# Scores of a batch cut into 14 pieces that fill their PSUM banks, in five bursts for six, and attention pairs released at four per MLP chunk

## The chip, the cores and the metric

The kernel runs on one core of one Trainium2 chip. The metric is the device time of one execution, in microseconds. Durations and waits come from one profiled execution of each kernel, taken by the hardware profiler.

## The reference

Attention with 16 extra "beacon" keys ahead of each head's own keys (8 batches, 8 heads, 576 queries, head size 64), and behind it an MLP with a squared relu over the 4608 tokens that come out of it:

```python
k_all = np.concatenate([beacon_k, k], axis=2)          # 592 keys
v_all = np.concatenate([beacon_v, v], axis=2)
scores = scale * np.matmul(q, k_all.transpose(0, 1, 3, 2))
causal[:, Nb:] = np.triu(np.ones((S, S), dtype=bool), k=1)
scores = np.where(causal, -1000000000.0, scores)
a = np.exp(scores - scores.max(-1, keepdims=True))
a /= a.sum(-1, keepdims=True) + 1e-09
x = np.matmul(a, v_all)          # then tokens x 512
h = x @ w_in                     # 512 -> 2048
r = np.maximum(h, 0.0)
out = (r * r) @ w_out            # 2048 -> 512
```

## The kernel before

The work of a batch is four head pairs; pair p = 4b + pr. The 592 keys make five key blocks c of 128 (the last has 80), and the queries five tiles t, of 112, 128, 128, 128 and 80 rows, so that block c meets the tiles from c on. Scores are made transposed, keys on the partitions: one matmul of TensorE per key block and head, with 64 rows of weights, and the two heads of a pair side by side in the upper and the lower half of the array. One such couple is called a step below. A tuple `(c, t0, t1, col)` in `WHOLE` is a step: key block c, queries t0 to t1, at column `col` of the PSUM bank (one bank for each head). The steps of one bank pair are a piece; ScalarE takes its exponential into the pair's tile `pt` in one instruction (L768). VectorE then masks the diagonal blocks with triangles from `tri` by a minimum (L783, and L787 for the block of 80), TensorE multiplies the probabilities by v (30 matmuls of 65 columns, L803; the 65th column gives the sum), and VectorE divides into `xn` (L818, L819).

Scores come in bursts: `SIZES` says how many pieces one scheduled operation takes, each with a bank pair of its own. In batch 0, split in two phases (`SPLIT`), it is one piece, in batch 1 two pieces, and from batch 2 on the 16 pieces of a batch make six bursts (3, 3, 3, 3, 2, 2).

When all four pairs of a batch are done, `xn` is turned into `xT` by five DMA transposes that SyncE issues (L850; batch 0 uses TensorE). The MLP takes tokens in nine chunks of 512: chunk j needs xT of the batches up to j, chunk 8 of batch 7. A chunk is 64 matmuls of 512 columns by w_in (L931), relu on ScalarE or VectorE (L948, L950), a square on VectorE (L957) and 64 matmuls by w_out (L968), which ScalarE copies out (L437) and SyncE stores (L991).

From batch 3 on, q and k are loaded by SyncE (L484, L483 for the beacons), cast by GpSimd, and turned into `qT` and `kT` by DMA transposes of SyncE (L516). The transposes, the loads and the stores stand in one queue. `qT`, `kT`, `xn` and the cast v have two buffers each, `pt` four.

The order of instructions on every engine is fixed when the kernel is built: the class `Order` plays the program through with assumed costs and always takes the operation with the lowest `prio` that may go. Attention comes ahead of the MLP, except that a pair is held back by its `gate` until the MLP has come far enough:

```python
mlp_chunk_us = 27.7
LEAD, PACE = -0.4, 0.225
return o.progress >= mlp_chunk_us * (LEAD + PACE * (p - HP))
```

Here `progress` is the MLP's TensorE time already given out, and HP is 4.

Of the kernel before, what the change touches and what calls it, by code (L numbers as in the profile page):

```python
# [10 lines left out]
BF16 = mybir.dt.bfloat16  # L11
AF = mybir.ActivationFunctionType
# [117 lines left out]
class Order:  # L130
# [180 lines left out]
def kernel(  # L311
# [29 lines left out]
    def sb(name, shape, dt):  # L341
        return pool.tile(shape, dt, name=name)

    NSTG, NPT, RB = 8, 4, 4
# [22 lines left out]
    pt = [sb(f"pt{i}", [128, 2, 2048], BF16) for i in range(NPT)]  # L367
# [7 lines left out]
    tri = sb("tri", [128, 4, 128], BF16)  # L375
# [8 lines left out]
    def act(n):  # L384
        return 0.066 + n / 1200.0
# [17 lines left out]
    add = order.add  # L403
# [8 lines left out]

    def add_pad(i):
        def emit(e):
            for lo, hi in ((928, 1024), (1440, 1536), (1824, 2048)):
                nc.vector.memset(pt[i][:, :, lo:hi], 0.0)

        return add(f"pad{i}", "DVE", 0.5, emit, prio=100.0 * i)
# [1 line left out]
    pads = [add_pad(i) for i in range(NPT)]  # L420

    def emit_tri(e):
        for i in range(4):
            nc.gpsimd.affine_select(out=tri[:, i, :], in_=tri[:, i, :], compare_op=ALU.is_ge, fill=0.0,
                                    base=Nb if i == 0 else 0, pattern=[[1, 128]], channel_multiplier=-1)
# [26 lines left out]
    def t_start(t):  # L452
        return max(0, 128 * t - Nb)
# [219 lines left out]
            self.lo = t_start(tiles[0])  # L673
            self.hi = t_start(tiles[-1]) + t_rows(tiles[-1])

    whole_off = {}
    for t in range(NT):
        for c in range(t + 1):
            whole_off[c, t] = ((t_start(t) if t < 4 else 1360) if c == 0 else
                               1744 if c == 4 else 512 * c + 128 * (t - c))  # L680
# [8 lines left out]
    SPLIT = [  # L689
        Phase(  # L690
            pieces=[([(0, 0, 240, 0), (1, 112, 240, 240)], 0, 368)],
            diag=(0, 240, 0, 2), last=None, tiles=range(0, 2), off={(0, 0): 0, (0, 1): 112, (1, 1): 240}),
        Phase(
            pieces=[
# [3 lines left out]
            ],  # L698
            diag=(512, 512, 2, 2), last=848, tiles=range(2, NT),
            off={(2, 2): 512, (2, 3): 640, (2, 4): 768, (4, 4): 848, (3, 3): 1024, (3, 4): 1152,  # L700
                 (0, 2): 1232, (0, 3): 1360, (1, 2): 1536, (1, 3): 1664, (1, 4): 1792, (0, 4): 1872}),
    ]
# [31 lines left out]
    def add_scores(pairs, n, sizes):  # L734

        work = [(x, i, piece) for x in pairs for i, piece in enumerate(phases(x.b)[n].pieces)]
        exps = {x.p: [] for x in pairs}
        at = 0
        for size in sizes:
            group = work[at:at + size]  # L740
            at += size
            prio = 100.0 * group[0][0].p + 1000.0 * n + group[0][1]
            cols = sum(t1 - t0 for _, _, (mms, _, _) in group for _, t0, t1, _ in mms)
            owners = list({x.p: x for x, _, _ in group}.values())
            box = {}

            def emit_qk(e, group=group, box=box):
                for k, (x, _, (mms, _, _)) in enumerate(group):
                    st = pair(box["qk"], k)
                    for c, t0, t1, col in mms:  # L750
                        for hj in range(2):
                            hp = slice(64 * hj, 64 * hj + 64)
                            nc.tensor.matmul(  # L753
                                st[:, hj, col:col + t1 - t0],
                                kT[x.b % 2][hp, x.pr, 128 * c:128 * c + 128],
                                qT[x.b % 2][hp, x.pr, t0:t1],
                                start=True, stop=True,
                            )

            qk = add(f"qk{group[0][0].p}.{n}.{group[0][1]}", "PE", cols / 2400.0, emit_qk, prio=prio,  # L760
                     deps=[d for x in owners for d in x.qk_deps + [x.take_pt]],
                     take=("ps", "late" if b < NSPLIT and n else "strip", [2] * size), gate=owners[0].gate, mode="rows")
            box["qk"] = qk
            for x in owners:
                qk_ops[x.p].append(qk)
            for k, (x, i, (_, off, width)) in enumerate(group):
                def emit_exp(e, off=off, width=width, k=k, x=x, box=box):
                    nc.scalar.activation(pt[x.take_pt.held[0]][:, :, off:off + width],  # L768
                                         pair(box["qk"], k)[:, :, 0:width], AF.Exp, bias=0.0, scale=scale)

                exps[x.p].append(add(f"exp{x.p}.{n}.{i}", "ACT", act(2 * width), emit_exp, prio=prio + 0.1 * k,
                                     deps=[qk], give=(qk, k)))
# [234 lines left out]
    late = []  # L1007
    for b in range(B):
        lp = 10.0 * b
        if b < NPE:  # L1010
            add_strided(b, lp - 200.0 if b == 0 else lp)
        if NPE <= b < NPE + 2:
            add_zero(b)
        v_loads[b] = []
        for n, (x, c) in enumerate(([] if b < NPE else nat) + [("v", c) for c in range(NT)]):
            behind, sync = [], []
            if x == "v" and b == 0:
                if c == 0:
                    sync = [strided[0][HP - 3, "q"]]
            elif x == "v" and b == 1 and c == 0:  # L1020
                behind = [strided[1][HP - 1, "q"]]
            elif b == 2 and n == 0:
                sync = [w_ops["out", 3]]
            add_load(b, x, c, lp + 0.1 * n, behind, sync)
            if x == "v":
                v_loads[b].append(load_chain[-1])
        if b >= NPE:
            add_trans(b, "k", lp - 5.0)
            add_trans(b, "q", lp - 5.1)
        if b == 0:  # L1030
            add_weights()
        if b == 1:
            add_weights_out()
        pairs = [add_pair(b, pr) for pr in range(HP)]
        if b < NSPLIT:
            for x in pairs:
                for n, ph in enumerate(phases(b)):
                    add_scores([x], n, [1] * len(ph.pieces))
        else:
            add_scores(pairs, 0, SIZES[b])  # L1040
# [48 lines left out]
```

## Time and profile before

| | |
|---|---|
| median of 3 runs | 343.65 us (343.54 to 343.87) |
| the profiled execution | 344.22 us |
| its span, first to last instruction | 342.4 us |
| TensorE matmuls busy | 325.1 us, 95% |
| ScalarE busy | 195.0 us, 57% |
| VectorE busy | 160.3 us, 47% |
| GpSimd busy | 81.1 us, 24% |
| matmuls of scores (L753) | 400 |
| granted TensorE clock | 1.0 |

Engines are PE (matmuls), PEld (weight loads, which overlap PE), DVE (VectorE), ACT (ScalarE), POOL (GpSimd) and SP (SyncE; with a q, its queue of DMA issues). A row of the timeline gives a start and a length in microseconds, the engine, the line, what is written and read, and how many instructions were merged; in brackets the idle time before it and what ended it. A matmul's length contains the time that its result takes to leave the array, so matmuls behind one another overlap in their rows, and the starts tell the pace. A row of the groups gives busy time and the mean length of one in ns, then the idle time before. In the waits it is who waited for whom: sum in us, times, the longest. A row of the stretches has the stretch and its length, the busy time and count of PE, PEld, DVE, ACT and POOL, the granted clock, the DMA engines' share and GB/s. A few records of matmuls are missing.

### The profile page before, as it was taken

Reading aid. Unit: us, or ns where it says so; the run is one execution under the profiler, and the core shown is the slowest. Engines: PE = TensorE matmul, PEld = TensorE weight load, DVE = VectorE, ACT = ScalarE, POOL = GpSimd, SP = SyncE. Lnnn points to the kernel's source line nnn. Section 1 sums busy time; section 2 is a strip of 40 time slices with the busy share of each in tenths; the row PEclk is TensorE's granted clock in tenths of the full one; section 3 lists DMA queues with packets and bytes.
Section 4 is the critical chain, followed back from the end, with each engine's and each line's share of the span. In section 5 each row is a group of like instructions: output and inputs, shape, how many; then the busy total and the mean of one; then the engine's idle time right before and its main releaser. Section 6 shows DMA issues by size and latency. Waiting matters only on the chain.

```text
span 342.4 us, 7074 instructions
## 1 busy us (share of the span) xinstructions
PE 325.1 (95%) x2838; PEld 175.7 (51%) x2876; DVE 160.3 (47%) x323; ACT 195.0 (57%) x301; POOL 81.1 (24%) x129
## 2 busy tenths in 40 slices
PE   2999999999999999999999799999999999999995
PEld 2677665454544544453557574444544444444442
DVE  6788978177425842385524483287403202301400
ACT  3987873588358564577554754597326326515611
POOL 6545802516124222423241126020000000000000
PEclk9999999999999999999999999999999999999999
DMA  9999999699979996999999889980041011011002
GB/s 166 197 205 221 206 204 208 134 252 204 188 164 215 197 199 145 255 188 224 133 209 220 184 177 207 219 170 24 15 117 63 0 61 63 0 61 63 0 29 93
DMA packets 139472, 50.33 MB, mean 147 GB/s; under 512 B 125808, under 2 KB 134512, under 8 KB 139440
## 3 DMA queue, kind: packets, MB, share of 16 engines
q1 hardware_dynamic: 129856, 40.91, 58.1%
q0 software_dynamic: 9376, 8.69, 15.5%
q8 instruction: 22, 0.36, 0.5%
q10 hardware_dynamic: 208, 0.29, 0.3%
q14 instruction: 10, 0.08, 0.1%
HBM read 37.22 MB, written 9.44 MB: 136 GB/s over the span
## 4 chain that ended last, share of the span: by engine, by line
PE 66%; DMA 19%; SPq 7%; DVE 4%; issue 2%; POOL 2%; ACT 1%; POOLq 0%; DVEq 0%; ACTq 0%
PE ps L931 28%; PE ps L968 26%; PE ps L803 5%; SPq L850 5%; PE ps L753 5%; DMA kT<-qk_area 5%; DMA stg<-in_k_dram 4%; DMA bks<-in_beacon_k_dram 3%; DMA stg<-in_v_dram 3%; DVE g L957 2%; DMA stg<-in_q_dram 1%; DMA qk_area<-in_q_dram 1%; SPq L484 1%; POOL w_in L892 1%; PE ps L635 1%
## 5 line engine op out<-in xcount | busy, mean ns | idle before, releaser
L931 PE MATMUL ps<-xT,w_in 128*128 128x512 bf16 (+3 forms) x688 | 134.3, 340 | 1.1 <-DMA xT<-xn 0.2
L968 PE MATMUL ps<-w_out,g 128*128 128x512 bf16 x554 | 127.9, 379 | 1.1 <-issue 0.2
L768 ACT ACTIVATE pt<-ps 128x832 bf16<-128x832 f32 (+4 forms) x128 | 102.9, 872 | 28.6 <-PE ps L753 28.5
L931 PEld LDWEIGHTS <-w_in 128*128 128x128 bf16 x704 | 64.9, 98 | 57.8 <-issue 7.7
L957 DVE TENSOR_TENSOR g<-g 128x1024 bf16<-128x1024 bf16 (+2 forms) x80 | 53.6, 673 | 76.9 <-ACT g L948 75.6
L948 ACT ACTIVATE g<-ps 128x512 bf16<-128x512 f32 (+2 forms) x117 | 66.3, 567 | 39.9 <-PE ps L931 39.2
L968 PEld LDWEIGHTS <-g 128*128 128x128 bf16 x576 | 54.1, 98 | 64.1 <-issue 2.9
L437 ACT COPY osb<-ps 128x512 f32<-128x512 f32 x36 | 21.3, 591 | 65.0 <-PE ps L968 60.4
L439 POOL CAST vb<-stg 128x512 bf16<-128x512 f32 (+1 forms) x36 | 24.3, 684 | 84.3 <-DMA stg<-in_v_dram 39.9
L439 POOL CAST qk_area<-stg 128x512 bf16<-128x512 f32 (+2 forms) x50 | 32.1, 645 | 50.6 <-DMA stg<-in_q_dram 33.8
L783 DVE TENSOR_TENSOR pt<-pt,tri 128x1024 bf16<-128x1024 bf16 (+1 forms) x36 | 23.9, 667 | 31.3 <-ACT pt L768 31.3
L803 PEld LDWEIGHTS <-pt 128*128 128x128 bf16 (+1 forms) x960 | 33.6, 98 | 7.6 <-issue 1.2
L950 DVE TENSOR_SCALAR g<-ps 128x512 bf16<-128x512 f32 (+2 forms) x43 | 25.7, 600 | 24.9 <-PE ps L931 24.5
L803 PE MATMUL ps<-vb,pt 128*128 128x65 bf16 (+1 forms) x960 | 34.9, 194 | 1.3 <-DVE pt L783 0.5
L753 PE MATMUL ps<-qT,kT 64*128 64x80 bf16 (+7 forms) x400 | 33.5, 282 | 2.6 <-DMA kT<-qk_area 2.1
L819 DVE TENSOR_TENSOR xn<-ps,rcp 128x640 bf16<-128x640 f32 (+2 forms) x36 | 27.0, 750 | 1.5 <-DVE rcp L818 0.2
L753 PEld LDWEIGHTS <-kT 64*128 64x128 bf16 x400 | 13.5, 96 | 23.2 <-issue 15.4
L818 DVE RECIPROCAL rcp<-ps 128x10 f32<-128x10 f32 (+2 forms) x36 | 7.5, 208 | 23.1 <-PE ps L803 23.0
L437 ACT COPY qT<-ps 128x576 bf16<-128x576 bf16 x12 | 7.5, 640 | 6.4 <-PE ps L635 5.0
L439 DVE COPY kT<-ps 128x576 bf16<-128x576 bf16 x12 | 8.9, 751 | 2.8 <-PE ps L638 1.9
L787 DVE TENSOR_TENSOR pt<-pt,tri 80x160 bf16<-80x160 bf16 x32 | 10.0, 312 | 0.0
L635 PE MATMUL ps<-ident,sparek 96*128 96x96 bf16 x18 | 1.5, 229 | 6.0 <-DVE sparek L439 6.0
(49 smaller groups left out, 71.7 us busy)
## 6 DMA issues: line engine op xcount, KB each, us to landing
out_dram<-osb SPq DMA_DIRECT2D x17, 512.0 KB, 3.3
stg<-in_v_dram SPq DMA_DIRECT2D x21, 256.0 KB, 5.0
stg<-in_q_dram SPq DMA_DIRECT2D x20, 256.0 KB, 4.7
stg<-in_k_dram SPq DMA_DIRECT2D x15, 256.0 KB, 5.1
w_in<-in_moe_w_in_dram POOLq DMA_DIRECT2D x4, 512.0 KB, 8.2
w_out<-in_moe_w_out_dram POOLq DMA_DIRECT2D x4, 512.0 KB, 10.9
stg<-in_v_dram SPq DMA_DIRECT2D x7, 224.0 KB, 4.2
qk_area<-in_k_dram POOLq DMA_DIRECT2D x4, 288.0 KB, 12.7
```

Of the source, the lines that this page charges most:

```text
L437: nc.scalar.copy(dst, src)
L439: eng[e].tensor_copy(dst, src)
L753: nc.tensor.matmul(st[:, hj, col:col + t1 - t0], kT[x.b % 2][hp, x.pr, 128 * c:128 * c + 128], qT[x.b % 2][hp, x.pr, t0:t1], start=True, s ...
L768: nc.scalar.activation(pt[x.take_pt.held[0]][:, :, off:off + width], pair(box["qk"], k)[:, :, 0:width], AF.Exp, bias=0.0, scale=scale)
L783: nc.vector.tensor_tensor(out=d, in0=d, in1=tri[:, m0:m0 + m, :][:, None].to_broadcast([128, 2, m, 128]), op=ALU.min)
L803: nc.tensor.matmul(a[:, hj, (t - tl[0]) * (D + 1):(t - tl[0] + 1) * (D + 1)], P[0:rr, hj, o:o + 128], vb[b % 2][0:rr, c, h, :], start=(c = ...
L819: nc.vector.tensor_tensor(out=xn[b % 2].rearrange("p t (h d) -> p h t d", d=D)[:, 2 * pr:2 * pr + 2, tl[0]:tl[0] + nt], in0=a[:, :, :, 0:D ...
L931: nc.tensor.matmul(h[:, lo - spans[0][0]:hi - spans[0][0]], w_in_sb[:, mc, ft * 128:(ft + 1) * 128], xT[:, mc, lo % RING:lo % RING + hi - lo],
L948: nc.scalar.activation(dst, h, AF.Relu, bias=0.0, scale=1.0)
L950: nc.vector.tensor_scalar(out=dst, in0=h, scalar1=0.0, scalar2=None, op0=ALU.max)
L957: nc.vector.tensor_tensor(out=d, in0=d, in1=d, op=ALU.mult)
L968: nc.tensor.matmul(o, G[:, fc, ts * 128:(ts + 1) * 128], w_out_sb[:, fc, :], start=(fc == 0), stop=(fc == NFT - 1))
```

## The change

Three things change. First, the pieces of a batch. A pair's 1664 score columns are cut into 512, 512, 512 and 128 where they were 496, 464, 416 and 288: all five key blocks' last 80 queries stand in one piece, in eleven steps a pair where there were six. From batch 2 on the pieces of 128 of pairs 0 and 1, and of pairs 2 and 3, share a bank pair, so that 14 bank pairs hold a batch; each still has its own exp, as it belongs to another `pt`. Second, these 14 make five bursts (3, 3, 3, 3, 2) where 16 made six. Batch 1 has the new cut, with eight bursts of two as before; batch 0 is as it was. Third, `PACE` goes from 0.225 to 0.25, so the gate lets four pairs go for each chunk of the MLP. What else changes follows from the new places in `pt`: a fifth triangle and shorter pads.

```diff
-            for lo, hi in ((928, 1024), (1440, 1536), (1824, 2048)):
+            for lo, hi in ((928, 1024), (1440, 1536), (1824, 2000)):
...
-        for i in range(4):
+        for i in range(5):
             nc.gpsimd.affine_select(...)
-                                    base=Nb if i == 0 else 0, ...)
+                                    base=Nb if i in (0, 4) else 0, ...)
...
     WHOLE = [Phase(
         pieces=[
-            ([(0, 0, 496, 0)], 0, 496),
-            ([(1, 112, 576, 0)], 512, 464),
-            ([(2, 240, 576, 0), (0, 496, 576, 336)], 1024, 416),
-            ([(3, 368, 576, 0), (4, 496, 576, 208)], 1536, 288),
+            ([(0, 0, 112, 0)] + [(c, 496, 576, 112 + 80 * c) for c in range(NT)], 1152, 512),
+            ([(1, 112, 496, 0), (3, 368, 496, 384)], 0, 512),
+            ([(0, 112, 368, 0), (2, 240, 496, 256)], 512, 512),
+            ([(0, 368, 496, 0)], 1024, 128),
         ],
-        diag=(0, 512, 0, 4), last=1744, tiles=range(NT), off=whole_off)]
+        diag=(0, 384, 1, 4), last=1584, tiles=range(NT), off={...})]
...
-    SIZES = {b: [2] * 8 if b < 2 else [3, 3, 3, 3, 2, 2] for b in range(B)}
+    ONE_BY_ONE = [[(x, i)] for x in range(HP) for i in range(4)]
+    SHARED = [[(0, 0)], [(0, 1)], [(0, 2)], [(0, 3), (1, 3)], [(1, 0)], [(1, 1)], [(1, 2)], [(2, 0)], [(2, 1)],
+              [(2, 2)], [(2, 3), (3, 3)], [(3, 0)], [(3, 1)], [(3, 2)]]
+    PIECES = {b: ONE_BY_ONE if b < 2 else SHARED for b in range(B)}
+    SIZES = {b: [2] * 8 if b < 2 else [3, 3, 3, 3, 2] for b in range(B)}
...
-    LEAD, PACE = -0.4, 0.225
+    LEAD, PACE = -0.4, 0.25
...
+                    for x, _, lo, (mms, _, _) in parts:
+                        for c, t0, t1, col in mms:
+                            for hj in range(2):
+                                nc.tensor.matmul(
+                                    st[:, hj, lo + col:lo + col + t1 - t0], ...)
...
+                    own.append(add(f"exp{x.p}.{n}.{i}", "ACT", act(2 * width), emit_exp, prio=prio + 0.1 * k,
+                                   deps=[qk], give=(qk, k) if len(parts) == 1 else None))
+                if len(parts) > 1:
+                    add(f"share{lead.p}.{n}.{k}", "-", 0.0, None, deps=own, give=(qk, k))
```

The order moves with it. SyncE's queue at batch 4's xT (L850, from `xn0`), with loads of batch 6 around it. Before:

```order
L483 DMA stg5_68<-in_beacon_k_dram 16x8x64
L484 DMA stg5_68<-in_k_dram 112x8x64
L484 DMA stg6_69<-in_q_dram 128x8x64
L850 DMA_TRANSPOSE xT_89<-xn0_85 128x4x112
L850 DMA_TRANSPOSE xT_89<-xn0_85 128x4x128 x3
L850 DMA_TRANSPOSE xT_89<-xn0_85 128x4x80
L484 DMA stg7_70<-in_q_dram 128x8x64
L484 DMA stg0_63<-in_q_dram 128x8x64
```

The same place now (L866 is the old L850, and the last row is the old L516, for batch 6):

```order
L484 DMA stg6_69<-in_q_dram 128x8x64
L484 DMA stg7_70<-in_q_dram 128x8x64
L484 DMA stg0_63<-in_q_dram 128x8x64
L484 DMA stg1_64<-in_q_dram 128x8x64
L484 DMA stg2_65<-in_k_dram 128x8x64
L484 DMA stg3_66<-in_q_dram 64x8x64
L484 DMA stg4_67<-in_k_dram 128x8x64
L866 DMA_TRANSPOSE xT_89<-xn0_85 128x4x112
L866 DMA_TRANSPOSE xT_89<-xn0_85 128x4x128 x3
L866 DMA_TRANSPOSE xT_89<-xn0_85 128x4x80
L516 DMA_TRANSPOSE qT0_77<-qk_area_71 128x20x128
```

The five transposes of xT have gone behind six more loads of q and k.

VectorE from the last normalisation of batch 4 (into `xn0`) on. Before, with `g1` the hidden layer of chunk 3:

```order
L818 RECIPROCAL rcp2_96<-ps_99 128x10
L819 TENSOR_TENSOR xn0_85<-ps_99,rcp2_96 128x2x5x64
L957 TENSOR_TENSOR g1_91<-g1_91 128x1024
L950 TENSOR_SCALAR g1_91<-ps_99 128x512
L957 TENSOR_TENSOR g1_91<-g1_91 128x1024
L950 TENSOR_SCALAR g1_91<-ps_99 128x512
L957 TENSOR_TENSOR g1_91<-g1_91 128x1024
L950 TENSOR_SCALAR g1_91<-ps_99 128x512
L957 TENSOR_TENSOR g1_91<-g1_91 128x1024
L783 TENSOR_TENSOR pt2_83<-pt2_83,tri_98 128x8x128
L787 TENSOR_TENSOR pt2_83<-pt2_83,tri_98 80x2x80
```

The same now (L834, L835, L799, L803 and L966 are the old L818, L819, L783, L787 and L950), with `g0` the hidden layer of chunk 4:

```order
L834 RECIPROCAL rcp2_96<-ps_99 128x10
L835 TENSOR_TENSOR xn0_85<-ps_99,rcp2_96 128x2x5x64
L799 TENSOR_TENSOR pt0_81<-pt0_81,tri_98 128x2x4x128
L803 TENSOR_TENSOR pt0_81<-pt0_81,tri_98 80x2x80
L834 RECIPROCAL rcp0_94<-ps_99 128x10
L835 TENSOR_TENSOR xn1_86<-ps_99,rcp0_94 128x2x5x64
L799 TENSOR_TENSOR pt1_82<-pt1_82,tri_98 128x2x4x128
L803 TENSOR_TENSOR pt1_82<-pt1_82,tri_98 80x2x80
L966 TENSOR_SCALAR g0_90<-ps_99 128x512
```

The first relu of chunk 4 on VectorE, which needs xT of batch 4, now comes seven instructions behind the batch's last normalisation; before, chunk 3 was still at its first layer there.

More of the change, by code (lines that the diff above doesn't have):

```diff
@@ L366 @@
     kT = [sb(f"kT{i}", [128, HP, NT * 128], BF16) for i in range(2)]
-    pt = [sb(f"pt{i}", [128, 2, 2048], BF16) for i in range(NPT)]
+    pt = [sb(f"pt{i}", [128, 2, 2000], BF16) for i in range(NPT)]
     xn = [sb(f"xn{i}", [128, NT, H * D], BF16) for i in range(2)]
@@ L374 @@
     rcp = [sb(f"rcp{i}", [128, 2, NT], FP32) for i in range(4)]
-    tri = sb("tri", [128, 4, 128], BF16)
+    tri = sb("tri", [128, 5, 128], BF16)
     ps = psum.tile([128, 8, 512], FP32, name="ps")
@@ L674, in __init__ @@
             self.hi = t_start(tiles[-1]) + t_rows(tiles[-1])
[L676 to L680, printed above, removed]
     WHOLE = [Phase(
         pieces=[
-            ([(0, 0, 496, 0)], 0, 496),
-            ([(1, 112, 576, 0)], 512, 464),
-            ([(2, 240, 576, 0), (0, 496, 576, 336)], 1024, 416),
-            ([(3, 368, 576, 0), (4, 496, 576, 208)], 1536, 288),
-        ],
-        diag=(0, 512, 0, 4), last=1744, tiles=range(NT), off=whole_off)]
+            ([(0, 0, 112, 0)] + [(c, 496, 576, 112 + 80 * c) for c in range(NT)], 1152, 512),
+            ([(1, 112, 496, 0), (3, 368, 496, 384)], 0, 512),
+            ([(0, 112, 368, 0), (2, 240, 496, 256)], 512, 512),
+            ([(0, 368, 496, 0)], 1024, 128),
+        ],
+        diag=(0, 384, 1, 4), last=1584, tiles=range(NT),
+        off={(0, 0): 1152, (0, 1): 512, (0, 2): 640, (0, 3): 1024, (1, 1): 0, (1, 2): 128, (1, 3): 256, (2, 2): 768,
+             (2, 3): 896, (3, 3): 384, (0, 4): 1264, (1, 4): 1344, (2, 4): 1424, (3, 4): 1504, (4, 4): 1584})]
     SPLIT = [
@@ L732, in __init__, with add_scores @@
             self.b, self.pr, self.p, self.take_pt, self.qk_deps, self.gate = b, pr, p, take_pt, qk_deps, gate
-    def add_scores(pairs, n, sizes):
-        work = [(x, i, piece) for x in pairs for i, piece in enumerate(phases(x.b)[n].pieces)]
+    def add_scores(pairs, n, sizes, pieces):
+        work = []
+        for shared in pieces:
+            at, parts = 0, []
+            for x, i in shared:
+                parts.append((pairs[x], i, at, phases(pairs[x].b)[n].pieces[i]))
+                at += parts[-1][3][2]
+            work.append(parts)
         exps = {x.p: [] for x in pairs}
@@ L741, in add_scores @@
             at += size
-            prio = 100.0 * group[0][0].p + 1000.0 * n + group[0][1]
-            cols = sum(t1 - t0 for _, _, (mms, _, _) in group for _, t0, t1, _ in mms)
-            owners = list({x.p: x for x, _, _ in group}.values())
+            lead = group[0][0][0]
+            prio = 100.0 * lead.p + 1000.0 * n + group[0][0][1]
+            every = [part for parts in group for part in parts]
+            cols = sum(t1 - t0 for _, _, _, (mms, _, _) in every for _, t0, t1, _ in mms)
@@ L745, in add_scores @@
+            owners = list({x.p: x for x, _, _, _ in every}.values())
             box = {}
             def emit_qk(e, group=group, box=box):
-                for k, (x, _, (mms, _, _)) in enumerate(group):
+                for k, parts in enumerate(group):
                     st = pair(box["qk"], k)
[L750 to L758, printed above, removed]
@@ L760, in add_scores @@
-            qk = add(f"qk{group[0][0].p}.{n}.{group[0][1]}", "PE", cols / 2400.0, emit_qk, prio=prio,
+                    for x, _, lo, (mms, _, _) in parts:
+                        for c, t0, t1, col in mms:
+                            for hj in range(2):
+                                hp = slice(64 * hj, 64 * hj + 64)
+                                nc.tensor.matmul(
+                                    st[:, hj, lo + col:lo + col + t1 - t0],
+                                    kT[x.b % 2][hp, x.pr, 128 * c:128 * c + 128],
+                                    qT[x.b % 2][hp, x.pr, t0:t1],
+                                    start=True, stop=True,
+                                )
@@ L761, in add_scores @@
+            qk = add(f"qk{lead.p}.{n}.{group[0][0][1]}", "PE", cols / 2400.0, emit_qk, prio=prio,
                      deps=[d for x in owners for d in x.qk_deps + [x.take_pt]],
-                     take=("ps", "late" if b < NSPLIT and n else "strip", [2] * size), gate=owners[0].gate, mode="rows")
+                     take=("ps", "late" if lead.b < NSPLIT and n else "strip", [2] * size), gate=lead.gate, mode="rows")
             box["qk"] = qk
@@ L765, in add_scores, with emit_exp @@
                 qk_ops[x.p].append(qk)
[L766 to L772, printed above, removed]
+            for k, parts in enumerate(group):
+                own = []
+                for x, i, lo, (_, off, width) in parts:
+                    def emit_exp(e, off=off, width=width, k=k, x=x, lo=lo, box=box):
+                        nc.scalar.activation(pt[x.take_pt.held[0]][:, :, off:off + width],
+                                             pair(box["qk"], k)[:, :, lo:lo + width], AF.Exp, bias=0.0, scale=scale)
+                    own.append(add(f"exp{x.p}.{n}.{i}", "ACT", act(2 * width), emit_exp, prio=prio + 0.1 * k,
+                                   deps=[qk], give=(qk, k) if len(parts) == 1 else None))
+                    exps[x.p].append(own[-1])
+                if len(parts) > 1:
+                    add(f"share{lead.p}.{n}.{k}", "-", 0.0, None, deps=own, give=(qk, k))
         assert at == len(work)
@@ L1037 @@
                 for n, ph in enumerate(phases(b)):
-                    add_scores([x], n, [1] * len(ph.pieces))
+                    add_scores([x], n, [1] * len(ph.pieces), [[(0, i)] for i in range(len(ph.pieces))])
         else:
-            add_scores(pairs, 0, SIZES[b])
+            add_scores(pairs, 0, SIZES[b], PIECES[b])
         if b < NXPE:
```

2 lines of the change are left out of this document (1 added, 1 removed).

## The prediction

> **What bounds the kernel now.** I read the page first, then busy time by stretches, the waits, the chain of waits, and last the timelines of TensorE (PE, with its weight loads PEld) and of SyncE's queue (SPq).
>
> ```profile
> span 342.4 us, 7074 instructions
> PE 325.1 (95%) x2838; PEld 175.7 (51%) x2876; DVE 160.3 (47%) x323; ACT 195.0 (57%) x301; POOL 81.1 (24%) x129
> DMA  9999999699979996999999889980041011011002
> PE 66%; DMA 19%; SPq 7%; DVE 4%; issue 2%; POOL 2%; ACT 1%; POOLq 0%; DVEq 0%; ACTq 0%
> 180.00:210.00 30.00, 27.88 (x290) 19.33 (x289) 16.40 (x27) 17.70 (x26) 7.62 (x13) 1.00 0.94 197
> 210.00:240.00 30.00, 29.73 (x274) 14.70 (x277) 16.35 (x30) 19.85 (x30) 4.96 (x8) 1.00 0.74 143
> 300.00:330.00 30.00, 29.84 (x138) 13.61 (x139) 5.53 (x8) 12.00 (x21) 0.00 (x0) 1.00 0.09 36
> ```
>
> PE is busy 95% of the span at a full clock (the 1.00 in the stretches), and for the rest only its start and one stretch stand out: from 180 to 210 it lacks 2.1 us. The DMA engines are full for the first 26 slices, some 225 us. So the end moves by what is taken from PE's own stream, by what PE waits for, and by nothing else. What it waits for:
>
> ```profile
> PE ps L753 <- DMA kT<-qk_area: 2.1, 1, 2.1
> PE ps L931 <- DMA xT<-xn: 0.2, 1, 0.2
> 148.36 7.67 DMA kT<-qk_area
> 182.54 7.74 DMA kT<-qk_area
> 190.32 0.76 PE ps L753 x8
> ```
>
> The two kT rows are pieces of the chain: the transposed keys of batch 5 and of batch 6 (the first is 0). The scores of batch 6 begin at 190.32, when its keys land; that is the 2.1 us. The loads are behind attention there. The wait for xT, which feeds the first MLP matmul of each chunk, is 0.2 us in all.
>
> **A burst's own cost.** PE's timeline around one burst of scores (L753), the third row being PEld:
>
> ```profile
> 205.27 1.03 PE L968 MATMUL ps<-w_out,g 128*128 128x512 bf16 x4
> 206.23 0.69 PE L753 MATMUL ps<-qT,kT 64*128 64x336 bf16 x10
> 206.22 0.38 PEld L753 LDWEIGHTS <-kT 64*128 64x128 bf16 x10 [0.42 <-issue]
> 206.85 3.63 PE L968 MATMUL ps<-w_out,g 128*128 128x512 bf16 x16
> 210.31 1.08 PE L803 MATMUL ps<-vb,pt 128*128 128x65 bf16 x30
> ```
>
> Sixteen 512-column matmuls take 210.31 - 206.85 = 3.46 us, 0.216 each. Four of them from 205.27 have streamed by 206.13, and the burst starts at 206.23: 0.10 lost going in. The burst holds five steps (both heads of a pair run side by side, so ten matmuls) of 336, 80, 208, 80 and 496 columns, 1200 in all: at 512 per 0.216 that is 0.506 us, and the next work starts 0.62 us after the burst's start: 0.11 lost inside and going out. So a burst costs 0.21 us over its columns, whatever it holds.
>
> **The change, part by part.**
> Batches 2 to 7 go from six bursts to five: 6 x 0.21 = **1.3 us off**. Batch 1 keeps eight.
>
> Columns stay at 1664 a pair, but in 11 steps where there were 6: the last 80 queries of all five key blocks make five steps of 80 in a row. That is 5 x 28 pairs = 140 more steps. Of the 0.11 us above, 0.10 is as much as going in cost, so the four further steps of that burst, two of them narrow, cost 0.01 to 0.02 together: at most 5 ns each, and at least none. I take 2.5 ns, the middle: **0.35 us on** (0 to 0.7).
>
> ScalarE's exps stay 16 a batch, of the same sum of elements:
>
> ```profile
> L768 ACT ACTIVATE pt<-ps 128x832 bf16<-128x832 f32 x36 | 31.2, 873 | 15.4 <-PE ps L753 15.3
> L768 ACT ACTIVATE pt<-ps 128x928 bf16<-128x928 f32 x32 | 30.5, 954 | 2.8 <-PE ps L753 2.8
> L768 ACT ACTIVATE pt<-ps 128x992 bf16<-128x992 f32 x28 | 28.1, 1003 | 7.5 <-PE ps L753 7.5
> L768 ACT ACTIVATE pt<-ps 128x576 bf16<-128x576 f32 x28 | 18.4, 658 | 2.9 <-PE ps L753 2.9
> ```
>
> Now 873 + 954 + 1003 + 658 = 3488 ns a pair. By (1003 - 658)/416 = 0.83 ns an element, three of 1024 are 3 x 1030 and one of 256 is 393: 3483. Nothing. The masks keep their sizes. GpSimd makes a fifth triangle, a quarter of the first row here, ahead of an idle time of 4.75 us:
>
> ```profile
> 5.61 1.49 POOL L424 TENSOR_SCALAR_AFFINE_SELECT tri<-tri 128x128 bf16<-128x128 bf16 x4
> 11.86 0.61 POOL L439 CAST vb<-stg 128x512 bf16<-128x512 f32 x1 [4.75 <-DMA stg<-in_v_dram]
> ```
>
> So those 0.37 us cost nothing either. The last exp of a pair now often belongs to the next burst, so a mask may come later to PE's probabilities-times-values matmuls (L803): between 0.5 us lost and, since some small waits of before will go, 0.5 won. I take 0.
>
> Pace. From batch 5's first burst to batch 6's, the order has 48 first-layer matmuls (L931) before and 64 now, the 64 second-layer ones as ever: 16 x 0.216 less one burst, 3.2 us more PE work per batch. From batch 2 to 6 attention comes about 4 x 3.2 = 12.8 us later against the loads. In SyncE's queue kT of batch 6 now stands behind three more rows, two v loads and a store:
>
> ```profile
> 158.74 0.66 SPq L484 DMA_DIRECT2D stg<-in_q_dram  x1
> 159.49 7.50 SPq L850 DMA_TRANSPOSE xT<-xn  x5
> 167.04 2.19 SPq L484 DMA_DIRECT2D stg<-in_q_dram  x3
> ...
> 177.56 4.25 SPq L516 DMA_TRANSPOSE qT<-qk_area  x1
> xT<-xn SPq DMA_TRANSPOSE x35, 2.5
> ```
>
> From 167.04 to 177.56 the queue passes ten loads (8 of q and k, 2 of v): 1.05 us each. So kT moves by some 3 us and its user by 12: **2.1 us off**, all of the wait (0 if the loads stay the pace, a rival below; 2.3 with the other small ones).
>
> What is late next: xT. It is issued when all four pairs of a batch are normalised, and the later release brings that closer to the chunk that needs it. From the end of the last L803 of batch 4 (154.06) to xT:
>
> ```profile
> 153.14 1.09 PE L803 MATMUL ps<-vb,pt 128*128 128x65 bf16 x30
> 154.06 1.89 PE L931 MATMUL ps<-xT,w_in 128*128 128x512 bf16 x7
> 244.97 1.24 PE L968 MATMUL ps<-w_out,g 128*128 128x512 bf16 x5
> 246.27 6.42 SPq L850 DMA_TRANSPOSE xT<-xn  x5
> 179.34 1.04 PE L931 MATMUL ps<-xT,w_in 128*128 128x256 bf16 x8
> ```
>
> Its five transposes are issued from 159.49 to 166.99; an issue takes about 1.25 us (6.42/5), and the last lands 2.5 us after its start: 168.2. That is 14.1 us after PE left the batch, with the queue full of loads; for batch 7, with it empty (PE goes on at 244.97, last issue ends at 252.69, landing 253.9), 9.0 us. Before, PE had other work until 179.3. In the new order it has, after the last L803 of batches 2, 3, 4 and 6, only 48 L968 matmuls (10.4 us), 30 of L803 (0.92) and three bursts (1536, 1280 and 1536 columns, 1.84, and 3 x 0.21): **13.8 us** for what took 14.1 at worst. Batch 5 has 16 matmuls more, 17.2; batch 7 has the 48 alone, 10.4 against 9.0. So chunk 4 misses by 0.3, the others hold. The absolute count agrees: SyncE comes to batch 4's xT six loads later, 159.4 + 6 x 1.05 = 165.7, landing 8.7 later at 174.4; by the order PE comes to chunk 4 earlier than 179.3 by two groups of L803 (1.84), 2304 columns (0.97) and three bursts (0.6) that now stand behind, and by some 0.5 won till then: 175.4. I put **0.5 us on** for all chunks (0 to 3).
>
> The sum: -1.3 + 0.35 - 2.1 + 0.5 = -2.55 us. The profiled execution took 344.22 us, 1.8 over its span, so it would take 341.67; it lies 0.57 over the median of the runs, 343.65, and the same difference from the median gives **341.1 us**. The ends of the terms give -4.1 (no narrow cost, no xT wait, 0.5 of other waits gone, 2.3) to +0.8 (0.7, 3, 0.5, and the 2.1 won): 339.5 to 344.5.
>
> **Rivals.**
> *xT becomes the bound (slower).* If SyncE reaches the transposes of chunks 3 and 4 half of the six loads later than I have it, 3.1 us, PE stands 3.4 us at the one (14.1 + 3.1 - 13.8; the other is then covered), and the 1.1 us by which the worst latency of the trace might pass 13.8 is lost again at chunk 2 or 6. That is 4.5 for my 0.5: 343.65 - 2.55 + 4.0 = 345.1. It ends slower, by over 0.7 us, once these waits pass 3.7. For it: all transposes share one queue with the loads, and the margins are under 2 us. Against it: the two counts above agree, and a stall of PE gives the next batch's loads time.
>
> *The loads stay the pace (no change).* kT is waited for as before, in another place, and only bursts and steps are won, less 0.5: 343.65 - 1.3 + 0.35 + 0.5 = 343.2. For it: DMA share 0.94 to the end of loading. Against it: 12 us of slack for 3 us of delay.
>
> *Narrow steps wait for their weights (slower).* A weight load of 64x128 lasts 96 ns in the trace, a step of 80 columns 34. If loads did not overlap, each of the 8 steps of at most 128 columns that a pair now has (768 columns, 320 ns) would last 96, as would 2 (160 columns, 67 ns) before: 448 - 125 = 323 ns x 28 = 9.0 us, so 341.1 - 0.35 + 9.0 = 349.8.
>
> ```profile
> L753 PEld LDWEIGHTS <-kT 64*128 64x128 bf16 x400 | 13.5, 96 | 23.2 <-issue 15.4
> ```
>
> Against it: in the burst above ten loads stand in 0.38 us, and the row of 30 L803 steps is over in 0.92, 31 ns a step with a load each. The Trainium skill, "TensorE: Matmul & The Clock Gate", section "Back-to-back issue gap", speaks against this change too: it gives a sustained stream of weight load and matmul pairs about 81 ns a matmul at 128 columns. By an estimate from that figure the 8 steps would cost 648 ns and the 2 before 162, a difference of 233 ns x 28 = 6.5 us over the columns, and the time would be 347.3. The 31 ns of the L803 row disagrees with it at 65 columns.
>
> **How the numbers follow.** A measurement of this kernel tells apart about 0.2%, 0.7 us. The forecast, with its own range 339.5 to 342.9, gets 0.77, since its two larger terms are read from rows and only the waits are open. xT as the bound gets 0.13, the loads as the pace 0.08, weight loads 0.02. So faster 0.77, same 0.08, slower 0.15. The range goes from 339.4 to 343.9: it takes in the loads' rival and leaves out the slower ones and a little below.
>
> **What would show it.** In the profile after: 38 bursts in batches 1 to 7 for 44 now, 680 matmuls of scores for 400, with steps of 80 columns about 35 ns apart; no wait of the scores for kT near the start of batch 6; waits of the first-layer matmuls for xT of under 1 us, at chunk 4 if anywhere; ScalarE's total unchanged; the last L803 well behind 245. I am wrong if waits for xT add up to over 3 us, if a burst with five 80-column steps takes 0.2 us over its columns more than the others, or if the kT wait is still there.

## The result, and the profile after

The changed kernel takes 340.2 us, the median of 5 runs (339.93 to 342.16), against 343.87 of the kernel before, five runs beside it (343.54 to 345.86): a ratio of 0.9918, with an interval of 0.9889 to 0.9948 (the two medians by themselves would give 0.9893). By the interval it is faster by 0.8%, 1.8 to 3.8 us. Measured twice more it gave 0.9945 (0.9914 to 0.9976) and 0.9907 (0.9875 to 0.9939). The forecast was 341.1.

First the page of the changed kernel; its profiled execution took 341.99 us:

```profile
span 340.2 us, 7620 instructions
PE 325.6 (96%) x3118; PEld 183.0 (54%) x3156; DVE 162.4 (48%) x324; ACT 195.1 (57%) x300; POOL 84.8 (25%) x130
DMA  8999999689968999799969997991310041011002
L764 PE MATMUL ps<-qT,kT 64*128 64x80 bf16 (+6 forms) x680 | 33.9, 236 | 0.5 <-ACT pt L781 0.4
```

The 680 matmuls of scores are there, ScalarE's total stands still (195.1 for 195.0), and the DMA engines are full for about as long as before. The span is 2.2 us shorter, though PE is busy for 0.5 us more: it waits less. The stretches, with the columns as before:

```profile
180.00:210.00 30.00, 29.84 (x328) 20.96 (x330) 12.82 (x23) 18.84 (x29) 10.78 (x16) 1.00 1.04 202
210.00:240.00 30.00, 29.83 (x284) 15.24 (x286) 16.16 (x28) 17.48 (x25) 4.34 (x6) 1.00 0.66 142
300.00:330.00 30.00, 29.84 (x137) 13.59 (x139) 5.53 (x8) 13.03 (x22) 0.00 (x0) 1.00 0.10 36
```

From 180 to 210 PE had lacked 2.1 us and now lacks 0.16, as in the other stretches shown. What PE still waits for, all that the view lists:

```profile
PE ps L635 <- DVE sparek L439: 6.1, 1, 6.1
PE ps L947 <- DVE g L966: 1.0, 2, 0.6
PE ps L984 <- issue: 0.8, 5, 0.2
PE ps L764 <- ACT pt L781: 0.4, 1, 0.4
```

There is no row for kT and none for xT. The 6.1 us lie at the start of the program and were 6.0 before. In SyncE's queue the issues that matter are these:

```profile
167.10 8.33 SPq L866 DMA_TRANSPOSE xT<-xn  x5
187.68 4.31 SPq L516 DMA_TRANSPOSE kT<-qk_area  x1
```

The first row is xT of batch 4, the second kT of batch 6. That kT lands 5.7 us after its issue, at 193.4. PE's timeline has the scores of batch 6 from 200.04 on:

```profile
70.12 2.19 PE L947 MATMUL ps<-xT,w_in 128*128 128x512 bf16 x9
...
176.61 1.04 PE L947 MATMUL ps<-xT,w_in 128*128 128x256 bf16 x8
...
200.04 0.84 PE L764 MATMUL ps<-qT,kT 64*128 64x112 bf16 x20
200.82 5.35 PE L984 MATMUL ps<-w_out,g 128*128 128x512 bf16 x23
206.10 0.73 PE L764 MATMUL ps<-qT,kT 64*128 64x128 bf16 x20
206.77 1.90 PE L984 MATMUL ps<-w_out,g 128*128 128x512 bf16 x8
```

The scores come 6.6 us after their keys. The first row is the first matmul of chunk 1, the second the first of chunk 4; both are used below. ScalarE's exps by shape:

```profile
L781 ACT ACTIVATE pt<-ps 128x1024 bf16<-128x1024 f32 x84 | 82.3, 1032 | 9.7 <-PE ps L764 9.7
L781 ACT ACTIVATE pt<-ps 128x256 bf16<-128x256 f32 x28 | 9.5, 387 | 6.2 <-PE ps L764 6.2
```

A pair takes 3 x 1032 + 387 = 3483 ns, the sum that the prediction had.

Single executions of one kernel differ by some us, and part of that is settled before chunk 1 begins. Chunk 1 starts at 70.12 here. In another execution of the same kernel (e9 below) it starts at 68.72:

```profile
68.72 2.84 PE L947 MATMUL ps<-xT,w_in 128*128 128x512 bf16 x12
```

That is 1.4 us between two executions of one kernel, and 1.8 us between this one and the profiled execution of before (68.32), which is why the gain of 3.7 in the medians shows as 2.2 in the spans. So traces are compared below from the first matmul of chunk 1 to the end: 274.04 us before; 270.06, 270.42 and 269.75 in the changed kernel's three traces.

### The profile page after: what moved, and what is told of

Read it like the earlier page. It is cut to its first block, busy times and chain, and to the rows that moved or that the text cites. A ratio compares the mean times of both kernels' runs of the same rounds, so it can differ in the third digit from the quotient of the medians.

```text
span 340.2 us, 7620 instructions
## 1 busy us (share of the span) xinstructions
PE 325.6 (96%) x3118; PEld 183.0 (54%) x3156; DVE 162.4 (48%) x324; ACT 195.1 (57%) x300; POOL 84.8 (25%) x130
## 4 chain that ended last, share of the span: by engine, by line
PE 90%; DVE 5%; issue 1%; DMA 1%; ACT 1%; ACTq 0%; DVEq 0%
PE ps L984 36%; PE ps L947 34%; PE ps L819 9%; PE ps L764 8%; DMA g<-in_k_dram 1%; DVE qk_area L439 1%; PE ps L638 1%; DVE g L973 1%; DVE g L966 1%; DVE kT L439 1%; ACT pt L781 1%; PE ps L635 1%; DVE xn L835 1%; PE ps L883 0%; PE ps L533 0%
## 5 line engine op out<-in xcount | busy, mean ns | idle before, releaser
L781 ACT ACTIVATE pt<-ps 128x1024 bf16<-128x1024 f32 (+3 forms) x128 | 102.5, 871 | 18.1 <-PE ps L764 17.8
L947 PEld LDWEIGHTS <-w_in 128*128 128x128 bf16 x704 | 65.9, 98 | 57.2 <-issue 5.3
L973 DVE TENSOR_TENSOR g<-g 128x1024 bf16<-128x1024 bf16 (+2 forms) x80 | 51.8, 651 | 71.4 <-ACT g L964 70.9
L439 POOL CAST qk_area<-stg 128x512 bf16<-128x512 f32 (+2 forms) x50 | 34.3, 692 | 68.4 <-DMA stg<-in_k_dram 42.3
L799 DVE TENSOR_TENSOR pt<-pt,tri 128x1024 bf16<-128x1024 bf16 (+1 forms) x36 | 24.4, 677 | 34.7 <-ACT pt L781 34.6
L439 POOL CAST vb<-stg 128x512 bf16<-128x512 f32 (+1 forms) x36 | 25.4, 721 | 60.9 <-DMA stg<-in_v_dram 57.4
L819 PEld LDWEIGHTS <-pt 128*128 128x128 bf16 (+1 forms) x960 | 34.2, 98 | 6.1 <-issue 0.4
L966 DVE TENSOR_SCALAR g<-ps 128x512 bf16<-128x512 f32 (+2 forms) x44 | 26.9, 611 | 19.7 <-PE ps L947 19.5
L819 PE MATMUL ps<-vb,pt 128*128 128x65 bf16 (+1 forms) x960 | 35.6, 195 | 0.1
L764 PE MATMUL ps<-qT,kT 64*128 64x80 bf16 (+6 forms) x680 | 33.9, 236 | 0.5 <-ACT pt L781 0.4
L764 PEld LDWEIGHTS <-kT 64*128 64x128 bf16 x680 | 19.0, 96 | 17.7 <-issue 14.9
L835 DVE TENSOR_TENSOR xn<-ps,rcp 128x640 bf16<-128x640 f32 (+2 forms) x36 | 27.0, 750 | 1.6 <-DVE rcp L834 0.2
L834 DVE RECIPROCAL rcp<-ps 128x10 f32<-128x10 f32 (+2 forms) x36 | 7.6, 210 | 27.4 <-PE ps L819 27.1
L803 DVE TENSOR_TENSOR pt<-pt,tri 80x160 bf16<-80x160 bf16 x32 | 10.3, 321 | 0.0
```

The source lines that it names most:

```text
L439: eng[e].tensor_copy(dst, src)
L764: nc.tensor.matmul(st[:, hj, lo + col:lo + col + t1 - t0], kT[x.b % 2][hp, x.pr, 128 * c:128 * c + 128], qT[x.b % 2][hp, x.pr, t0:t1], sta ...
L799: nc.vector.tensor_tensor(out=d, in0=d, in1=tri[:, m0:m0 + m, :][:, None].to_broadcast([128, 2, m, 128]), op=ALU.min)
L819: nc.tensor.matmul(a[:, hj, (t - tl[0]) * (D + 1):(t - tl[0] + 1) * (D + 1)], P[0:rr, hj, o:o + 128], vb[b % 2][0:rr, c, h, :], start=(c = ...
L835: nc.vector.tensor_tensor(out=xn[b % 2].rearrange("p t (h d) -> p h t d", d=D)[:, 2 * pr:2 * pr + 2, tl[0]:tl[0] + nt], in0=a[:, :, :, 0:D ...
L947: nc.tensor.matmul(h[:, lo - spans[0][0]:hi - spans[0][0]], w_in_sb[:, mc, ft * 128:(ft + 1) * 128], xT[:, mc, lo % RING:lo % RING + hi - lo],
```

## The experiments

The first four share one comparison, in which the kernel before took 342.58 us.

**e1: the pace alone.** The kernel before with the new release of pairs:

```diff
-    LEAD, PACE = -0.4, 0.225
+    LEAD, PACE = -0.4, 0.25
```

> The kernel before with PACE 0.25 and nothing else: the old pieces, six bursts. My theory (pace takes the wait for kT of batch 6, bursts and steps are a separate gain): 2.1 us under the kernel before, about 341.6, and no wait of the scores for kT over 0.5 us. Rival (what was won came from the fuller pieces and the fewer bursts, the pace only moved attention): within 0.5 us of the kernel before, 343.5.

340.84 us, a ratio of 0.995 (0.9923 to 0.9978): 1.74 off, between 0.8 and 2.6. The waits of scores and of L803 in its trace:

```profile
PE ps L803 <- DVE pt L783: 0.5, 1, 0.5
PE ps L753 <- ACT pt L768: 0.4, 1, 0.4
```

No row has kT. From chunk 1 on it takes 270.72 us, 3.3 less than before. The later release takes the wait away by itself.

**e2: the new cut and the five bursts alone.** The changed kernel at the old pace:

```diff
-    LEAD, PACE = -0.4, 0.25
+    LEAD, PACE = -0.4, 0.225
```

> The changed kernel with PACE back at 0.225: the new pieces and five bursts alone. My theory: the wait for kT of batch 6 is still there, 2 to 3 us, since loads pace it, and it swallows what the bursts of batches 2 to 5 win ahead of it; 0.4 to 1 us under the kernel before, 343. Rival (the pieces carry the gain): 340.2 to 340.7, and little wait for kT.

347.47 us, a ratio of 1.014 (1.0097 to 1.0183): 4.9 slower than before, where a little under it was expected. PE's timeline shows the place:

```profile
229.53 0.44 PE L819 MATMUL ps<-vb,pt 128*128 128x65 bf16 x9
233.75 0.43 PE L819 MATMUL ps<-vb,pt 128*128 128x65 bf16 x5 [3.77 <-POOL vb L439]
```

The last tiles of v of batch 7 are late. SyncE's queue says why:

```profile
219.70 0.57 SPq L484 DMA_DIRECT2D stg<-in_v_dram  x1
220.37 6.48 SPq L866 DMA_TRANSPOSE xT<-xn  x5
226.95 1.48 SPq L1007 DMA_DIRECT2D out_dram<-osb  x1
228.48 1.76 SPq L484 DMA_DIRECT2D stg<-in_v_dram  x2
```

Two loads of v stand behind five transposes and a store, 8.2 us (228.48 - 220.27). In the kernel before, the same loads stood ahead of them:

```profile
219.34 3.21 SPq L484 DMA_DIRECT2D stg<-in_v_dram  x3
222.65 6.43 SPq L850 DMA_TRANSPOSE xT<-xn  x5
```

With the new cut at the old pace the planner puts xT ahead of these loads. kT cost only 0.3 us here. So the loads can bind at v as well as at kT, and what the new cut is worth depends on the pace that it meets.

The wait costs more than its own length. The stretches around its end, the clock in the third column from the right:

```profile
229.00:233.50 4.50, 0.92 (x12) 0.54 (x11) 1.39 (x2) 2.03 (x3) 0.42 (x1) 1.00 0.87 208
233.50:237.00 3.50, 3.10 (x26) 1.86 (x26) 1.05 (x2) 0.00 (x0) 0.78 (x2) 0.51 0.00 0
237.00:240.00 3.00, 2.95 (x31) 1.40 (x31) 0.97 (x2) 2.62 (x4) 0.00 (x0) 1.00 0.00 0
```

For some 3.4 us the granted clock is half, and matmuls of 512 columns start 0.43 us apart where they started 0.216 apart: 1.7 us lost. From chunk 1 on e2 takes 276.07 us, 5.7 to 6.3 more than the changed kernel's three traces. The waits for v (3.9) and kT (0.3) and the half clock (1.7) make 5.9 of that. All six runs of e2 have a mean clock of 0.993 to 0.995, which fits such a stretch in each of them.

**e3 and e4: six bursts against five, at the new cut and pace.** e4 is the changed kernel again, e3 has:

```diff
-    SIZES = {b: [2] * 8 if b < 2 else [3, 3, 3, 3, 2] for b in range(B)}
+    SIZES = {b: [2] * 8 if b < 2 else [3, 3, 2, 2, 2, 2] for b in range(B)}
```

> The changed kernel with its 14 pieces in six bursts a batch (3, 3, 2, 2, 2, 2) for five. My theory (a burst costs 0.21 us over its columns): 6 x 0.21 = 1.3 us over the changed kernel, 341.5. Rival (going in and out of a burst is hidden by other waits, or gives waits of as much elsewhere): within 0.4 us of the changed kernel.

> The changed kernel once more, beside the three above: 340.2, some 3.5 us under the kernel before. Its profile shows whether the 1.9 us by which its first profiled execution lay over its median fall before the first chunk that needs xT (some 70 us into the span), as a rival has it that puts them down to the start's loads, or behind, as waits of the new order: the first matmul of chunk 1 would then stand near 70.1 again.

e3 took 342.24 us, a ratio of 0.9988 (0.9959 to 1.0016), and e4 340.5, 0.9945 (0.9914 to 0.9976): 1.74 between the medians, though the intervals overlap. e4 is 2.1 under the kernel before here, where some 3.5 was expected. From chunk 1 on the traces have 270.81 and 270.42; without e4's one larger wait there (0.53 us for xT) they lie 0.92 apart, and e3 lies 1.06 over e9, the changed kernel's third trace, which has no such wait. So six bursts are worth 0.9 to 1.7, and the forecast was 1.3.

The price of the steps comes from the bursts alone: each from its first instruction to the first of the work behind it, less its columns at 0.216 us for 512. From chunk 1 on that is 3.81 us in e1 (34 bursts, 138 steps) and 4.03 in e3 (34 bursts, 246 steps). 108 more steps cost 0.22 us, 2.0 ns each.

e4's wait for xT is the one that the forecast had put at chunk 4. PE's timeline:

```profile
175.26 0.60 PE L947 MATMUL ps<-xT,w_in 128*128 128x256 bf16 x4
176.38 0.60 PE L947 MATMUL ps<-xT,w_in 128*128 128x256 bf16 x4 [0.53 <-DMA xT<-xn]
```

And SyncE's queue:

```profile
169.12 8.59 SPq L866 DMA_TRANSPOSE xT<-xn  x5
```

The third of the five by itself, from a window that holds it alone:

```profile
173.84 1.26 SPq L866 DMA_TRANSPOSE xT<-xn  x1
```

PE goes on at 176.38, before the last issue ends at 177.71, so it cannot have waited for all five. The trace has the landings too: the third transpose lands 2.50 us after its start, at 176.34, 0.04 before PE goes on, the fourth at 177.65 and the last at 178.82. Chunk 4 takes 512 tokens where a batch has 576, so of batch 4 it holds the first 256 and of batch 3 the rest: it needs three of the five pieces of 112, 128, 128, 128 and 80.

**e5 and e6: the pace further on, and less far.** These, e7 and e8 share a comparison with 344.55 us for the kernel before.

```diff
-    LEAD, PACE = -0.4, 0.25
+    LEAD, PACE = -0.4, 0.27      (e5; 0.24 in e6)
```

> The changed kernel with PACE 0.27, so that attention comes still later. By its order PE has 2.4 us of work between the last values matmul of batch 6 and the first matmul of chunk 6, 5.2 at chunk 7 and 8.5 at chunk 3, for 13.8, 10.4 and 13.8 in the changed kernel. Theory A, as in the prediction (a chunk's first matmul waits for all five transposes, 9.0 us behind the batch with an empty queue): waits for xT of 6.6 and 3.8 us at chunks 6 and 7 alone, 5 at chunk 3, over 12 us slower than the changed kernel. Theory B (chunk 6 reads tokens of the first two transposes only, chunk 7 of the first, chunk 3 of the first three; each comes 1.25 us before the next): 2.7 us at chunk 6, none at chunk 7, 2 to 3 at chunk 3; 4 to 7 us slower than the changed kernel.

> The changed kernel with PACE 0.24, between 0.225 (347.5) and 0.25 (340.5). PE has 18 to 29 us of other work between a batch and its chunk, so no wait for xT. If the loads' pace is what 0.225 meets, a part of that wait comes back: 0.5 to 3 us over the changed kernel. Rival (0.225 only met one bad order of SyncE's queue, v behind xT): within 0.5 us of the changed kernel.

e5 took 352.31 us, a ratio of 1.0227 (1.0182 to 1.0272). e6 took 341.39, 0.9926 (0.9902 to 0.995), and no wait of PE behind the start passes 0.5 us there. It lies 1.4 over e8 below, which is of the same comparison, but from chunk 1 on its trace has 270.16, as the changed kernel's have; e11 against e10, both with the old cut in batch 1, give the two paces the same time. e5's waits:

```profile
PE ps L947 <- DMA xT<-xn: 3.9, 2, 3.4
PE ps L764 <- ACT pt L781: 2.6, 5, 0.6
```

PE's timeline at the two places:

```profile
143.12 2.89 PE L947 MATMUL ps<-xT,w_in 128*128 128x512 bf16 x8 [3.39 <-DMA xT<-xn]
...
252.45 0.40 PE L764 MATMUL ps<-qT,kT 64*128 64x256 bf16 x4 [0.52 <-ACT pt L781]
253.37 0.29 PE L764 MATMUL ps<-qT,kT 64*128 64x128 bf16 x4 [0.52 <-ACT pt L781]
```

SyncE's queue at the first:

```profile
135.77 8.06 SPq L866 DMA_TRANSPOSE xT<-xn  x5
```

At the first place the scores of a batch are over and the MLP stands for xT, 3.4 us. At the second no MLP work lies between the scores, and each of them waits for ScalarE to empty a bank. PE again goes on (143.12) before the last of the five issues is over (143.83), and 0.04 us after the third has landed (143.08). The smaller wait for xT (0.54 us, before 214.61, at chunk 5) ends 0.13 after the second landing, and chunk 5 reads two pieces. The clock is halved here as well:

```profile
143.90:147.30 3.40, 3.40 (x27) 1.35 (x25) 0.62 (x2) 1.85 (x5) 0.00 (x0) 0.50 0.83 158
```

So neither theory had the sum. Chunk 3 waited 3.4 us, nearer to B's 2 to 3 than to A's 5. Of A's 6.6 and 3.8 at chunks 6 and 7 and B's 2.7 at chunk 6 nothing came: the second piece for chunk 6 lands at 254.99, and PE, held up by ScalarE, comes to the chunk only at 255.53. That the time is A's "over 12 us" is chance. From chunk 1 on the trace takes 279.02 us, 9.0 more than the changed kernel's first. The waits for xT (3.9), ScalarE (2.6) and `xn` (0.6) and the half clock (1.7) make 8.8 of it; neither theory had ScalarE or the clock. The traced execution took 349.67 us. The other three took 352.04 to 352.73 with a mean clock of 0.985 to 0.990 for 0.995, and none of them has a trace.

With e2 this makes a window. At 0.225 the new cut loses by its loads, at 0.24 and 0.25 nothing larger is waited for, and at 0.27 xT and ScalarE cannot follow.

**e7: what a narrow step costs.** Every step of 80 columns in the full first piece of a pair cut into two of 40 (a part of the line is shown):

```diff
-    [(c, 496, 576, 112 + 80 * c) for c in range(NT)]
+    [(c, t, t + 40, 112 + 80 * c + t - 496) for c in range(NT) for t in (496, 536)]
```

> The changed kernel with each step of 80 columns cut into two of 40, nothing else: the same columns and the same order, 140 more steps. By the prediction's price (2.5 ns a step): 0.35 us over the changed kernel. Rival (a weight load must be over before the next step begins, and one takes some 34 ns, as long as 80 columns): two steps of 40 columns take 68 ns for 35, 140 x 33 ns = 4.6 us over it. Between, 28 ns a step as the shortest steps of the trace have it: 140 x 21 ns = 2.9 us.

342.48 us, a ratio of 0.9959 (0.9924 to 0.9995). The same two bursts as above, by PE's timeline:

```profile
200.15 0.91 PE L764 MATMUL ps<-qT,kT 64*128 64x112 bf16 x30
200.99 5.35 PE L984 MATMUL ps<-w_out,g 128*128 128x512 bf16 x23
206.28 0.80 PE L764 MATMUL ps<-qT,kT 64*128 64x128 bf16 x30
207.01 1.90 PE L984 MATMUL ps<-w_out,g 128*128 128x512 bf16 x7
```

They take 0.84 and 0.73 us where the changed kernel's took 0.78 (200.04 to 200.82) and 0.67: 0.06 us for five more steps (ten more matmuls), 12 ns each. Over all bursts from chunk 1 on it is 5.21 us less columns, where the changed kernel has 3.43 and 3.58 in two traces: 1.63 to 1.78 for 115 more steps, 14 to 15 ns each. Steps of 80 columns start 35 ns apart, so one of 40 takes about (35 + 14)/2 = 24.5 ns, where half the columns' time would be some 17. Read singly, the 40-column steps of e7 start 25 ns apart. So neither the 0.35 us that the prediction's price would give nor the rival's 4.6 came: 140 more steps at 14 to 15 ns are about 2 us, nearest to the 2.9 between the two. At 80 columns the steps still go at the pace of the columns (0.216 us x 80/512 = 34 ns); at 40 something else holds them, and what it is was not tested.

**e8 to e11: the cut of batch 1, and the pace beside it.** e8 and, repeated, e10 leave batch 1 in its old cut, with its pieces 496 columns apart in `pt`; e11 has that and the pace of 0.24. e9 is the changed kernel a third time, in the same comparison as e10 and e11 (343.57 us before).

```diff
-        return SPLIT if b < NSPLIT else WHOLE
+        return SPLIT if b < NSPLIT else OLD if b == 1 else WHOLE
```

> The changed kernel with the old cut of the pieces in batch 1 alone (its columns in the tile of probabilities close together, 496 apart); all from batch 2 on stays. If the new cut costs batch 1 something, as the first matmul of chunk 1 suggests (68.7 to 70.1 us with the new cut in four profiles, 68.3 and 69.0 with the old in two): 0.3 to 1 us under the changed kernel, and that matmul near 68.5. Rival (these are chances of the first loads): the same as the changed kernel.

> The changed kernel a third time, to stand beside the next two on one chip. 2 to 3.7 us under the kernel before, as in its two earlier comparisons.

> The changed kernel with the old cut in batch 1, again. If the new cut costs batch 1 something: 0.3 to 1 us under the changed kernel. Rival (chance of the start): within 0.3 us of it. From the first weights-turning matmul near 32 us to the first matmul of chunk 1 it took 36.7 in its first profile, and 36.4 to 37.6 in seven with the new cut.

> The same with PACE 0.24. If 0.24 has nothing left to gain over 0.25 (no wait of over 0.5 us for kT, v or xT in either): within 0.4 us of the one above. If attention coming earlier leaves the last chunks freer: 0.3 us faster; if loads pace it again: slower by up to 2.

e8 took 340.03 us, 0.9888 (0.9857 to 0.9918). Beside each other, e9 took 340.18, 0.9907 (0.9875 to 0.9939), e10 340.48, 0.9934 (0.9907 to 0.9961), and e11 340.37, 0.9911 (0.9881 to 0.9941). They are the same. With the old cut in batch 1 chunk 1 starts at 68.45, 69.45 and 68.08 us in e8, e10 and e11, with the new one at 70.12, 69.09 and 68.72: the ranges overlap. The late chunk 1 of the first trace is thus put down to its execution and not to the new cut, and none of these versions beats the changed kernel.

**e12: the kernel before, once more,** to see whether its wait comes again.

> The kernel before, for a second profile. My theory: the wait of the scores for kT of batch 6, or for another load of batches 5 to 7, is there again at 1 to 3 us, and from the first matmul of chunk 1 to the end it takes 273 to 275 us, for 270 in the changed kernel. Rival (that wait was one profile's chance): under 0.5 us of waits for loads, and 271.5.

One execution, 345.05 us. Its waits for loads:

```profile
PE ps L803 <- POOL vb L439: 1.8, 1, 1.8
PE ps L753 <- DMA kT<-qk_area: 1.8, 1, 1.8
```

kT is waited for again, 1.8 us for 2.1, and this time v too. From chunk 1 on this execution takes 275.0 us. The slack tells the same: in the two traces of the kernel before, the scores of batches 5, 6 and 7 start 0.05 to 1.44 us after their keys land, in the three of the changed kernel 1.6 to 8.7 us after. That the loads pace the kernel before is so in both of its traces; by how much, and where, changes from one to the next.

## Why the prediction was right, and where its steps were not

**The total.** 340.2 us for 341.1, within the range, and faster as forecast. The signs that it named came: 680 matmuls of scores, no wait for kT, xT waited for at chunk 4 or nowhere (0, 0.53 and 0 us in three traces), ScalarE unchanged, the last multiplication by v at 268.7 us for 245. The forecast gain, 2.55 us, lies among the 3.7, 2.1 and 3.4 that the medians of three comparisons give.

**Pace and kT (-2.1).** Right, and shown by e1, which has this part alone: -1.74 by the medians, with 2.1 inside the interval. The traces from chunk 1 on show more, 3.3 us, since the later release also removed smaller waits, such as 0.5 us of L803 for `xn` of VectorE. Two numbers on the way were off: kT was issued 5.1 us later (187.68 for 182.54) where I had some 3, and its user came 9.7 later (200.04 for 190.32) where I had about 12. The margin came out at 6.6 us instead of 9 or so, and one trace flatters it: in e4 the keys of batch 6 land at 197.76 and their scores start at 199.38, in e9 at 195.60 and 198.32, so it was 1.6 and 2.7 us there. It was wide enough in all three, but not by much.

**Bursts (-1.3) and steps (+0.35).** Right. The 0.21 us a burst, read from one burst, gave 1.3 for six, and e3 against e4 and e9 gives 0.9 to 1.7. Steps cost 2.0 ns each for the 2.5 taken, 0.28 us for 140. The rival in which narrow steps wait for their weights is out: e7 would have cost far more than 14 ns a step if a load of 96 ns stood in the open. The changed kernel's steps of 128 columns, a weight load with each matmul, start 55 to 56 ns apart in its traces; that disagrees with the 81 ns a matmul at 128 columns of the Trainium skill ("TensorE: Matmul & The Clock Gate", section "Back-to-back issue gap"). The same section's floor of about 25 ns for the smallest matmuls agrees with the 24.5 ns of e7.

**xT (+0.5): the right place, by a wrong premise and some luck.** I had SyncE reach the transposes of batch 4 at 165.7 and PE come to chunk 4 at 175.4. It was 167.1 and 176.6 in the first trace, 169.1 and 175.3 in e4. In e4 the queue was thus 3.4 us later than I had it, which is the condition of the slower rival (3.1), and by my premise, that a chunk waits for all five transposes, PE, which came to the chunk at 175.26, would have stood until the last one landed at 178.82, over 3 us. It stood 0.53, because chunk 4 needs only the first three, and e4's third landed at 176.34. The step that failed is "the last lands 2.5 us after its start": the last one does not matter. The margin was wider than I gave it, and the rival's price of 4 us was too high at this pace. That the 0.5 us was met in one trace of three is luck: a queue later than I had it and a need smaller than I had it nearly cancelled. The rival's mechanism is real all the same: at a pace of 0.27 the waits for xT and the half clock behind the longer one (3.9 and 1.7 us) are more than the gain.

**The sum.** I added the terms as if each stood by itself. The four corners in one comparison say no: 342.58 with neither part, 340.84 with the pace, 347.47 with cut and bursts, 340.5 with both. Cut and bursts are +4.9 us at the old pace. At the new one they bring 0.34 by the medians, whose intervals overlap, and 0.3 to 1.0 by the traces from chunk 1 on. So most of the gain is the pace's; that the rest of it is more than nothing rests on the bursts counted in the traces and on e3 against e4. The prediction read kT and xT from the order of the whole change, so its total stands without the corners; but its terms do not say what each edit is worth alone, since the planner writes a new queue for each combination.

**What stays open.** Why executions of the kernel before spread from 340.95 to 344.99 us in one comparison is not settled. Its two traces have 2.1 and 3.6 us of waits for kT and v; whether its shortest executions have none was not seen. That a long wait brings the half clock about rests on two traces, e2 and e5.

## What to carry to other kernels

Where a planner writes the order, price a combination of edits from the order that it gives, and measure the corners: a part that costs 4.9 us alone can be worth something beside another. A rate that holds back one stage has a window with an edge on either side, here loads that come late below it and a missing input above it; look for what waits at each edge, not for the best value between them. Price a long wait of TensorE by the granted clock behind it too. Before you count a transfer as late, ask which pieces of it the first consumer reads.

## What the runs showed of the hardware

A step of 40 columns took about 25 ns from start to start, one of 80 took 35: halving a step saved 10 ns and not 17. Issuing a transpose of xT from SyncE mostly took 1.26 us, also beside loads, but one or two of five then took 1.7 to 2.9 (2.90 in e4, 2.83 in e5): 6.42 us for five in a quiet queue, 8.06 and 8.59 where the queue of loads was full. So a queue's length cannot be counted in issues alone.

Behind the two longest waits of TensorE from chunk 1 on, 3.77 us in e2 and 3.39 us in e5, the granted clock stood at 0.5 for 3.4 us. Behind the waits of 1.8 to 2.1 us in the two traces of the kernel before it stayed at 1.00.
